# A linear-attention and gated-MLP kernel: the spatial products of the last batch as seven half-block products in place of eight

## The chip, the core and the metric

The kernel runs on one core of one Trainium2 chip. The metric is device time in microseconds: 328.46 (median of three runs, 327.94 to 328.81). One execution was also taken with the hardware profiler; it took 327.86 us.

## The reference

Four batches of 1088 tokens go through linear attention with four heads and then through a gated MLP in which the tokens are mixed. The MLP's input is the attention's output `x` of one batch, 1088 tokens x 128 channels:

```python
h = gelu(x @ w_in)                      # 1088 x 1024
u, v = h[..., :512], h[..., 512:]
v_n = (v - mean(v)) / sqrt(var(v) + 1e-6) * g_ln
v_s = einsum('ts,bsd->btd', w_sg, v_n) + b_sg[None, :, None]    # the spatial product
out = x + (u * v_s) @ w_out
```

The spatial product takes the weights `w_sg` (1088 x 1088), the same for all batches, times the normalized half `v_n` (1088 x 512). It is most of the arithmetic.

## The kernel before

All matrix products of the MLP are made from two-word numbers: each factor is held as a high word (a cast to `fp32r`) and a low word (what the cast left), and a product is three TensorE matmuls, high x high, high x low and low x high. In the names `w_h`, `w_l` are the words of the transposed spatial weights, `vh`, `vl` those of the normalized values.

**Tiles.** The 1088 input tokens are nine tiles `t` of 128 (the last is half full and is used as one matmul per word of the values). The 1088 output tokens are three chunks `ci` of 362, 362 and 364 columns (`CH`, line 23). The 512 gate features are four blocks `db` of 128. One spatial product of a block and a chunk, `pz_db_ci`, gathers in one PSUM bank over the nine tiles: 8 x 3 + 2 = 26 matmuls (`zs`, line 854). Batch 3 has 12 of them. Then follow, for each block and chunk, `gt` = z * g_ln + bias (`scale`, line 873, VectorE, one operand in PSUM), the product with `u` (`gate`, 882, VectorE), its two words `gh` (`g_h`, 886, ScalarE) and `gl` (`g_l`, 891, VectorE) and three matmuls into `po` (`out`, 904). `pu` (line 859) is the product for `u`, `pv` (717 to 744) that for the values; `vn` are the values, `v3` (line 815) normalizes a tile on ScalarE, `split_h` and `split_l` (823, 829) make the two words of a block, the first on ScalarE and the second on VectorE.

**Attention of batch b+1** runs beside the MLP of batch b. The names that matter here: `pk`, `pkv` and `pnd` are its matmuls; `kv_h`, `kv_l` the words of the key-value sums (lines 437, 439, VectorE), which `pnd` needs as weights; `e_0a`, `e_0b` and so on hold the query features, whose words are `qph` (ScalarE, line 509) and `qpl` (line 514). `qpl` is GpSimd's only regular work: six subtractions of two SBUF tiles for each of the batches 1 to 3.

**What sets the order.** The program is a list of about 1700 steps made by the functions at the end of the file. `WHEN` (line 36) holds one number for each step, and the steps are written into the program in the order of these numbers (`Steps.run`, line 137). Each engine then works through its own instructions in this order; semaphores between engines are set by the tiles that the steps write and read. Nothing is reordered at run time: an instruction that waits holds back all that stand behind it on its engine.

Of the kernel before, what the change touches and what calls it, by code (L numbers as in the profile page):

```python
# [120 lines left out]
]  # L121


def f32(ap):
# [4 lines left out]


# [993 lines left out]
```

## Time and profile before

| | |
|---|---|
| median of three runs | 328.46 us |
| profiled execution | 327.86 us |
| span of that execution, first to last instruction | 325.8 us |
| TensorE matmuls busy | 318.4 us, 98% of the span |
| VectorE, ScalarE, GpSimd busy | 251.6, 158.8, 22.8 us |
| granted TensorE clock | 1.0 of full speed throughout |

The last batch's spatial products start at 259 us of the span; the MLP of batch 2 and the attention of batch 3 run before and beside them. A busy PE means that matmuls are in its pipe: consecutive ones overlap, so the step from one start to the next is the better measure of what one costs.

### The profile page before, as it was taken

Reading aid. Unit: us, or ns where it says so; the run is one execution under the profiler, and the core shown is the slowest. Engines: PE = TensorE matmul, PEld = TensorE weight load, DVE = VectorE, ACT = ScalarE, POOL = GpSimd, SP = SyncE. Lnnn points to the kernel's source line nnn. Section 1 sums busy time; section 2 is a strip of 40 time slices with the busy share of each in tenths; the row PEclk is TensorE's granted clock in tenths of the full one; section 3 lists DMA queues with packets and bytes.
Section 4 is the critical chain, followed back from the end, with each engine's and each line's share of the span. In section 5 each row is a group of like instructions: output and inputs, shape, how many; then the busy total and the mean of one; then the engine's idle time right before and its main releaser. Section 6 shows DMA issues by size and latency. Waiting matters only on the chain.

```text
span 325.8 us, 5961 instructions
## 1 busy us (share of the span) xinstructions
PE 318.4 (98%) x2282; PEld 304.7 (93%) x2282; DVE 251.6 (77%) x614; ACT 158.8 (49%) x347; POOL 22.8 (7%) x35
## 2 busy tenths in 40 slices
PE   7999999999999999999999999999999999999995
PEld 5777999899999999999999999999999999999993
DVE  5899999999998967597988967768998874443243
ACT  4579714646549734354629815244634954131210
POOL 0300000022200000202200000112200000000000
PEclk9999999999999999999999999999999999999999
DMA  7999934774000115832000012551000000000002
GB/s 218 370 423 348 404 137 131 175 180 118 2 0 0 48 49 138 194 96 57 2 0 24 2 68 47 109 94 45 2 1 2 24 35 11 0 2 0 0 2 68
DMA packets 14091, 29.55 MB, mean 91 GB/s; under 512 B 1744, under 2 KB 10224, under 8 KB 13680
## 3 DMA queue, kind: packets, MB, share of 16 engines
q1 hardware_dynamic: 13344, 23.87, 25.1%
q0 software_dynamic: 720, 5.31, 4.3%
q8 instruction: 18, 0.29, 0.4%
q14 instruction: 9, 0.07, 0.1%
...
## 4 chain that ended last, share of the span: by engine, by line
PE 82%; DVE 11%; ACT 3%; DMA 2%; issue 1%; SPq 1%; ACTq 0%; DVEq 0%
PE pz L840 38%; PE pz L849 17%; PE pu L864 3%; DVE w_l L708 2%; PE po L913 2%; PE pu L866 2%; PE po L911 2%; PE pu L865 2%; PE po L910 2%; PE pkv L420 2%; PE pv L736 2%; PE pv L735 2%; PE pv L744 2%; DMA vn<-in_q 2%; PE pk L388 1%
## 5 line engine op out<-in xcount | busy, mean ns | idle before, releaser
L840 PE MATMUL pz<-w_h,vl 128*128 128x362 f32 (+1 forms) x432 | 140.1, 325 | 0.4 <-DVE vl L832 0.4
L840 PE MATMUL pz<-w_h,vh 128*128 128x362 f32 (+1 forms) x432 | 140.1, 325 | 0.0
L849 PE MATMUL pz<-w_l,vh 128*128 128x362 f32 (+1 forms) x384 | 118.0, 324 | 0.0
L840 PEld LDWEIGHTS pz<-w_h,vl 128*128 128x128 f32 x432 | 81.1, 188 | 1.4 <-DVE vl L832 0.9
L840 PEld LDWEIGHTS pz<-w_h,vh 128*128 128x128 f32 x432 | 81.1, 188 | 1.0 <-ACT u L871 0.3
L849 PEld LDWEIGHTS pz<-w_l,vh 128*128 128x128 f32 x384 | 71.1, 188 | 0.1
L877 DVE SCALAR_TENSOR_TENSOR gt<-pz,vi,b_bc 128x362 f32<-128x362 f32 (+3 forms) x49 | 28.5, 584 | 38.6 <-PE pz L840 38.3
L889 ACT CAST gh<-gt 128x362 fp32r<-128x362 f32 (+1 forms) x47 | 23.0, 493 | 53.6 <-DVE gt L884 49.8
L871 ACT ACTIVATE u<-pu 128x362 f32<-128x362 f32 (+1 forms) x48 | 22.7, 472 | 24.6 <-PE pu L866 16.2
L892 DVE TENSOR_TENSOR gl<-gt,gh 128x362 fp32r<-128x362 f32 (+1 forms) x47 | 26.4, 563 | 9.8 <-ACT gh L889 9.7
L827 ACT CAST vh<-vn 128x128 fp32r<-128x128 f32 (+1 forms) x72 | 25.8, 403 | 13.8 <-PE pz L840 13.4
L832 DVE TENSOR_TENSOR vl<-vn,vh 128x128 fp32r<-128x128 f32 (+1 forms) x72 | 28.5, 419 | 2.0 <-ACT vh L827 1.8
L817 ACT ACTIVATE vn<-vn,nm,rs 128x512 f32<-128x512 f32 x36 | 28.2, 811 | 2.6 <-DVE nm L811 2.5
L884 DVE TENSOR_TENSOR gt<-gt,u 128x362 f32<-128x362 f32 (+3 forms) x49 | 25.9, 528 | 0.9
L749 ACT ACTIVATE vn<-pv 128x512 f32<-128x512 f32 x36 | 21.0, 597 | 8.6 <-PE pv L744 7.7
L765 DVE BATCH_NORM_STATS2 st<-vn 128x6 f32<-128x512 f32 x33 | 22.5, 683 | 2.9 <-ACT vn L749 2.4
L535 DVE RECIPROCAL den<-den 128x362 f32<-128x362 f32 (+1 forms) x9 | 21.8, 2417 | 2.9 <-ACT den L530 2.9
L514 POOL TENSOR_TENSOR qpl<-e_0a,qph 128x362 fp32r<-128x362 f32 x6 | 6.5, 1103 | 145.2 <-ACT qph L509 145.2
L864 PE MATMUL pu<-x_h,win_h 128*128 128x362 f32 (+1 forms) x48 | 16.2, 338 | 0.0
L866 PE MATMUL pu<-x_l,win_h 128*128 128x362 f32 (+1 forms) x48 | 15.7, 327 | 0.0
L865 PE MATMUL pu<-x_h,win_l 128*128 128x362 f32 (+1 forms) x48 | 15.6, 326 | 0.0
L913 PE MATMUL po<-gl,wout_h 128*128 128x362 f32 (+1 forms) x47 | 15.5, 329 | 0.0
...
## 6 DMA issues: line engine op xcount, KB each, us to landing
...
```

The costliest lines, as they stand in the source:

```text
L765: V.bn_stats(st, self.vn[:, t])
L817: A.activation(self.vn[:, t], self.vn[:, t], AF.Identity, bias=self.nm[:, t : t + 1], scale=self.rs[:, t : t + 1])
L827: A.copy(self.parts[db][0][:, ts], self.vn[:, ts, P * db : P * db + P])
L832: V.tensor_sub(vl[:, ts], self.vn[:, ts, P * db : P * db + P], f32(vh[:, ts]))
L840: mm(self.z[db, ci], lhsT=self.parts[db][i][:, t], rhs=T["w_h"][:, t, AT[ci] : AT[ci] + cw], start=(t == 0 and i == 0), stop=(t == NT - 1 ...
L849: mm(self.z[db, ci], lhsT=self.parts[db][0][:, t], rhs=T["w_l", t][:, AT[ci] : AT[ci] + CH[ci][1]], start=False, stop=False,)
L864: mm(pu, lhsT=T["win_h"][:, ws], rhs=xh[:, cs], start=True, stop=False)
L871: A.activation(self.u[db, ci], self.pu.pop((db, ci)), AF.Gelu_apprx_tanh)
L877: V.scalar_tensor_tensor(self.gt[db, ci][:, s], self.z[db, ci][:, s], T["g_col"][:, db : db + 1], T["b_bc"][:, c0 : c0 + cw][:, s], op0=AL ...
L884: V.tensor_mul(gt, gt, self.u[db, ci][:, s])
L889: A.copy(self.g[db, ci][0], self.gt[db, ci])
L892: V.tensor_sub(self.g[db, ci][1], self.gt.pop((db, ci)), f32(self.g[db, ci][0]))
```

## The change

Batch 3 gets a class of its own, `Fast`, in place of `Gate`. For its blocks 0 and 2, and again for 1 and 3 (`PAIRS`), the tiles 0 to 3 and 4 to 7 and the chunks 0 and 1 make a product of two 2 x 2 matrices of half blocks (four tiles, one block, 362 columns: 12 matmuls each). Before, this took eight half-block products; now it is seven, of sums of half blocks, in Winograd's form of Strassen's method. The parts are:

- Sums of the weights (`Sums`): four for each of four tile pairs, `t1` to `t4`. The pieces of the weights are loaded anew from HBM by twelve DMAs on SyncE's queue (`ldT`), GpSimd makes the sums (`sum`, 16 instructions `T`), ScalarE their high words (`high`, 16) and GpSimd their low words (`rest`, 16). `t1` is stored over chunk 1 of tiles 0 to 3 in `w_h` and `w_l`; the others use tiles of the attention that are free by then.
- Sums of the values: `s1` to `s4` for each pair, on VectorE and in place in `vn` (`sums`, 8 instructions), and their words.
- The words of the values are made by half blocks (`word_h`, `word_l`) and for tile 8 alone (`edge`).
- The products `x`, `v`, `w`, `u` gather in one bank each. VectorE takes a bank out between (`take`: bank * g_ln + what was gathered before, which lies in SBUF), ten times for a pair, where `scale` stood four times.
- Chunk 2 (`third`) and tile 8 (`rest` of `Fast`) are as before in number.
- The order is new from the 1137th step on, in the middle of batch 2's MLP: the numbers in `WHEN` from the 1109th on are others; here one line of them.

```diff
+PAIRS = ((0, 2), (1, 3))
...
-    1116, 1119, 1121, 1125, 1128, 1192, 1051, 1088, 1118, 1122, 1124, 1127, 1129, 1132, 1133, 1135, 1136, 1138,
+    1116, 1119, 1121, 1125, 1128, 1273, 1051, 1088, 1118, 1122, 1124, 1127, 1129, 1132, 1133, 1135, 1153, 1159,
...
+    class Fast(Gate):
...
+        def word_h(self, j, n, t0, k):
+            A.copy(self.block(j, n)[:, 0, t0 : t0 + k], self.source(j, n)[:, t0 : t0 + k])
+
+        def word_l(self, j, n, t0, k):
+            w = self.block(j, n)
+            V.tensor_sub(w[:, 1, t0 : t0 + k], self.source(j, n)[:, t0 : t0 + k], f32(w[:, 0, t0 : t0 + k]))
+
...
+        def sums(self, j, n):
+            d1, d2 = PAIRS[j]
+            a11, a12, a21, a22 = (self.half(d, k) for d in (d1, d2) for k in range(2))
+            o, x, y, op = {
+                "s1": (a22, a21, a22, ALU.add), "s3": (a21, a11, a21, ALU.subtract),
+                "s2": (a22, a22, a11, ALU.subtract), "s4": (a12, a12, a22, ALU.subtract),
+            }[n]
+            V.tensor_tensor(o, x, y, op=op)
+
...
+        def product(self, j, o, left, right, t, first):
+            p = self.open((j, o))[:, : CH[0][1]]
+            w = self.words[j, left]
+            h, l = self.right(right, t)
+            mm(p, lhsT=w[:, 0, t], rhs=h, start=first, stop=False, **GO)
+            mm(p, lhsT=w[:, 0, t], rhs=l, start=False, stop=False, **GO)
+            mm(p, lhsT=w[:, 1, t], rhs=h, start=False, stop=t == 3, **GO)
+
+        def rest(self, j, o, db, ci):
+            p = self.open((j, o))[:, : CH[0][1]]
+            for i in range(2):
+                mm(
+                    p, lhsT=self.words[db][:, i], rhs=T["w_h"][:, NT - 1, AT[ci] : AT[ci] + CH[ci][1]],
+                    start=False, stop=i == 1, **GO,
+                )
+
+        def take(self, j, o, db, ci, first, final):
+            c0, cw = CH[ci]
+            z, add = self.open((j, o))[:, :cw], T["b_bc"][:, c0 : c0 + cw]
+            if not first:
+                add = self.acc[db, ci]
+            if final:
+                to = self.gt[db, ci] = new([P, CW], "gt", f"gt{self.b}_{db}_{ci}")[:, :cw]
+            elif first:
+                i = db // 2 if ci else 2
+                to = self.acc[db, ci] = T["vx"].rearrange("p n c -> p (n c)")[:, WP * i : WP * i + cw]
+            else:
+                to = add
+            V.scalar_tensor_tensor(to, z, T["g_col"][:, db : db + 1], add, op0=ALU.mult, op1=ALU.add)
+
...
+    class Sums:
...
+        def load(self, t, u):
+            if u == 0:
+                self.raw[t] = new([P, 3 * WP], "kld", f"wr{t}")
+                load(self.raw[t][:, : 2 * WP], wd[:, t, : 2 * WP])
+            elif u == 1:
+                load(self.raw[t][:, 2 * WP :], wd[:, t + 4, WP : 2 * WP])
+            else:
+                self.raw[t, 3] = new([P, WP], "wa", f"wa{t}")
+                load(self.raw[t, 3], wd[:, t + 4, :WP])
+
...
+        def sum(self, n, t):
+            x, y, op = {
+                "t3": ("b22", "b12", ALU.subtract), "t1": ("b12", "b11", ALU.subtract),
+                "t2": ("t3", "b11", ALU.add), "t4": ("b21", "t2", ALU.subtract),
+            }[n]
+            G.tensor_tensor(self.of(n, t), self.of(x, t), self.of(y, t), op=op)
+
...
+        def high(self, n, t):
+            if n == "t1":
+                cs = slice(AT[1], AT[1] + CH[1][1])
+                T[n, t] = T["w_h"][:, t, cs], T["w_l", t][:, cs]
+            else:
+                T[n, t] = [w[:, : CH[0][1]] for w in self.place(n, t)]
+            A.copy(T[n, t][0], self.of(n, t))
+
+        def rest(self, n, t):
+            h, l = T[n, t]
+            G.tensor_sub(l, self.of(n, t), f32(h))
...
     def gated(g, db, ci):
         if (db, ci) == g.final:
             return last(g, db, ci)
-        at(("gt", g.b, db, ci), lambda: g.scale(db, ci))
+        if not (isinstance(g, Fast) and ci < 2):
+            at(("gt", g.b, db, ci), lambda: g.scale(db, ci))
         at(("gm", g.b, db, ci), lambda: g.gate(db, ci))
         at(("gh", g.b, db, ci), lambda: g.g_h(db, ci))
         at(("gl", g.b, db, ci), lambda: g.g_l(db, ci))
...
+    def fast(g):
+        w = Sums()
+        for t in range(4):
+            for u in range(3):
+                at(("ldT", t, u), lambda t=t, u=u: w.load(t, u))
+            for n in ("t3", "t1", "t2", "t4"):
+                at(("T", n, t), lambda n=n, t=t: w.sum(n, t))
+            for n in ("t3", "t2", "t4"):
+                at(("Th", n, t), lambda n=n, t=t: w.high(n, t))
+                at(("Tl", n, t), lambda n=n, t=t: w.rest(n, t))
+        for t in range(4):
+            at(("Th", "t1", t), lambda t=t: w.high("t1", t))
+            at(("Tl", "t1", t), lambda t=t: w.rest("t1", t))
+        def pair(j, d1, d2):
+
+            def words(n, step):
+                for t in range(0, 4, step):
+                    at(("vh", g.b, j, n, t), lambda t=t: g.word_h(j, n, t, step))
+                    at(("vl", g.b, j, n, t), lambda t=t: g.word_l(j, n, t, step))
+
+            def products(o, left, right, first):
+                for t in range(4):
+                    at(("p", g.b, j, o, left, t), lambda t=t: g.product(j, o, left, right, t, first and t == 0))
+
+            def taken(o, db, ci, first=False, final=False):
+                if final:
+                    at(("gt", g.b, db, ci), lambda: g.take(j, o, db, ci, first, True))
+                    gated(g, db, ci)
+                else:
+                    at(("tk", g.b, j, o, db, ci), lambda: g.take(j, o, db, ci, first, False))
+
+            def rest(o, db, ci):
+                at(("p8", g.b, j, o, db, ci), lambda: g.rest(j, o, db, ci))
+
+            def third(db):
+                unit(g, db, 2)
+                for t in range(NT):
+                    at(("z", g.b, db, 2, t), lambda t=t: g.third(db, t))
+                gated(g, db, 2)
+
+            a11, a12, a21, a22 = ((d, k) for d in (d1, d2) for k in range(2))
+            for n in (a11, a12):
+                words(n, 4 if j else 1)
+            at(("vh", g.b, j, 8, d1), lambda: g.edge_h(d1))
+            at(("vl", g.b, j, 8, d1), lambda: g.edge_l(d1))
+            third(d1)
+            products("x", a11, (0, 0), True)
+            for n in (a21, a22):
+                words(n, 4)
+            at(("vh", g.b, j, 8, d2), lambda: g.edge_h(d2))
+            at(("vl", g.b, j, 8, d2), lambda: g.edge_l(d2))
+            for db, ci in ((d1, 1), (d2, 0), (d2, 1)):
+                taken("x", db, ci, first=True)
+            products("x", a12, (1, 0), False)
+            rest("x", d1, 0)
+            unit(g, d1, 0)
+            taken("x", d1, 0, first=True, final=True)
+            if not j:
+                third(d2)
+            products("v", a22, "t4", True)
+            rest("v", d2, 0)
+            taken("v", d2, 0)
+            at(("s", g.b, j, "s1"), lambda: g.sums(j, "s1"))
+            words("s1", 4)
+            for n in ("s3", "s2", "s4"):
+                at(("s", g.b, j, n), lambda n=n: g.sums(j, n))
+            words("s4", 4)
+            products("w", "s1", "t1", True)
+            taken("w", d2, 1)
+            products("w", "s4", (1, 1), False)
+            rest("w", d1, 1)
+            taken("w", d1, 1)
+            words("s2", 4)
+            products("u", "s2", "t2", True)
+            unit(g, d1, 1)
+            taken("u", d1, 1, final=True)
+            words("s3", 4)
+            products("u", "s3", "t3", False)
+            unit(g, d2, 0)
+            taken("u", d2, 0, final=True)
+            rest("u", d2, 1)
+            unit(g, d2, 1)
+            taken("u", d2, 1, final=True)
+            if j:
+                third(d2)
+
+        for j, (d1, d2) in enumerate(PAIRS):
+            pair(j, d1, d2)
...
     for b in range(1, B):
         attend(b)
-        g = Gate(b)
+        g = (Fast if b == B - 1 else Gate)(b)
         normed(g, GROUPS[1])
         if b == B - 1:
             for i in range(4):
                 at(("prep", i), lambda i=i, g=g: g.prepare(i))
-        main(g, 0)
+        if b == B - 1:
+            fast(g)
+        else:
+            main(g, 0)
```

On TensorE this is a stretch of batch 3 before, with `pu` of block 0 and chunk 1, the end of batch 2's last product and the first triple of batch 3's first one:

```order
L864 MATMUL pu_0_1_3353<-x_h,win_h 128x362
L865 MATMUL pu_0_1_3353<-x_h,win_l 128x362
L866 MATMUL pu_0_1_3353<-x_l,win_h 128x362
L840 MATMUL pz_3_2_3290<-w_h,vh_3_2869 128x364
L840 MATMUL pz_3_2_3290<-w_h,vl_3_2870 128x364
L840 MATMUL pz_0_0_3364<-w_h,vh_0_3307 128x362
L840 MATMUL pz_0_0_3364<-w_h,vl_0_3308 128x362
L849 MATMUL pz_0_0_3364<-w_l_710,vh_0_3307 128x362
```

And this is what stands behind the same `pu` now (`wb` are words of half blocks of values, `wt1t4` the words of sum `t4` of tile pair 1):

```order
L872 MATMUL pu_0_1_3520<-x_h,win_h 128x362
L873 MATMUL pu_0_1_3520<-x_h,win_l 128x362
L874 MATMUL pu_0_1_3520<-x_l,win_h 128x362
L1010 MATMUL pz_(0, 'x')_3354<-w_h,wb_04_3344 128x362
L1011 MATMUL pz_(0, 'x')_3354<-w_l_737,wb_04_3344 128x362
L1012 MATMUL pz_(0, 'x')_3354<-w_h,wb_04_3344 128x362
L1010 MATMUL pz_(0, 'v')_3461<-wt1t4h,wb_06_3422 128x362
L1011 MATMUL pz_(0, 'v')_3461<-wt1t4l,wb_06_3422 128x362
L1012 MATMUL pz_(0, 'v')_3461<-wt1t4h,wb_06_3422 128x362
L1010 MATMUL pz_(0, 'w')_3509<-w_h,wb_0s_3487 128x362
L1011 MATMUL pz_(0, 'w')_3509<-w_l_668,wb_0s_3487 128x362
L1012 MATMUL pz_(0, 'w')_3509<-w_h,wb_0s_3487 128x362
```

A product is still three matmuls of 362 columns; the products of several banks now take turns, triple by triple.

GpSimd's list from the attention of batch 3 to the end, before (`MEMSET kv` clears the key-value sums):

```order
L429 MEMSET kv_2724 128x256
L514 TENSOR_TENSOR qpl_0_2793<-e_0a,qph_0_2792 128x362
L514 TENSOR_TENSOR qpl_1_2826<-e_0a,qph_1_2825 128x362
L514 TENSOR_TENSOR qpl_2_2916<-e_1a,qph_2_2915 128x362
L514 TENSOR_TENSOR qpl_3_2961<-e_1a,qph_3_2960 128x362
L514 TENSOR_TENSOR qpl_4_3006<-e_2a,qph_4_3005 128x364
L514 TENSOR_TENSOR qpl_5_3052<-e_2a,qph_5_3051 128x364
```

And the same place now (`wr`, `wa` and `vi` hold pieces and sums of the weights, line 1095 makes a sum and line 1120 a low word):

```order
L439 MEMSET kv_2697 128x256
L1095 TENSOR_TENSOR wr_2581<-wr_2581 128x362
L1095 TENSOR_TENSOR vi<-wr_2581 128x362
L524 TENSOR_TENSOR qpl_1_2772<-e_0a,qph_1_2771 128x362
L524 TENSOR_TENSOR qpl_0_2784<-e_0a,qph_0_2783 128x362
L1095 TENSOR_TENSOR wr_2581<-wr_2581 128x362
L1120 TENSOR_TENSOR wt0t3l_2769<-wr_2581,wt0t3h 128x362
L524 TENSOR_TENSOR qpl_3_2877<-e_1a,qph_3_2876 128x362
L1120 TENSOR_TENSOR wt0t2l_2883<-wr_2581,wt0t2h 128x362
L524 TENSOR_TENSOR qpl_2_2864<-e_1a,qph_2_2863 128x362
L1095 TENSOR_TENSOR wa_2874<-wa_2874,wr_2581 128x362
L1095 TENSOR_TENSOR wr_2965<-wr_2965 128x362
```

The 32 new subtractions and additions of two SBUF tiles stand between the six of the attention and behind them; the last of them is read a little past the middle of batch 3's products.

VectorE's list at the key-value words of batch 3, before:

```order
L437 CAST kv_h<-kv_2724 128x256
L476 TENSOR_TENSOR ab_1_2654<-pab_1_2603,ab_1_2654 64x362
L439 TENSOR_TENSOR kv_l<-kv_2724,kv_h 128x256
L832 TENSOR_TENSOR vl_2_2594<-vn_2030,vh_2_2593 128x384
L458 TENSOR_TENSOR qt_2l<-q_2_2307,qt_2h 128x364
```

And now, with the two feature products `e_1a`, `e_0a` and the gating of block 0's chunk 2 between the two words:

```order
L447 CAST kv_h<-kv_2697 128x256
L513 TENSOR_TENSOR e_1a<-e_1a,e_1b 128x362
L513 TENSOR_TENSOR e_0a<-e_0a,e_0b 128x362 x2
L885 SCALAR_TENSOR_TENSOR gt_0_2_2790<-pz_0_2_2678,vi,b_bc 128x364
L840 TENSOR_TENSOR vl_2_2781<-vn_2031,vh_2_2780 128x384
L892 TENSOR_TENSOR gt_0_2_2790<-gt_0_2_2790,u_0_2_2498 128x364
L885 SCALAR_TENSOR_TENSOR gt_1_2_2812<-pz_1_2_2609,vi,b_bc 128x364
L486 TENSOR_TENSOR ab_2_2761<-pab_2_2754,ab_2_2761 64x364
L449 TENSOR_TENSOR kv_l<-kv_2697,kv_h 128x256
```

`kv_l` moved behind seven other instructions, and on TensorE the first `pnd` that reads it stands 24 matmuls behind the last one of `pz_0_2`, whose bank the `gt_0_2` row takes.

## Rows read from the trace of the kernel before

**Rows 1.** The page: busy us of each engine, share of the span, instructions.
```profile
PE 318.4 (98%) x2282; PEld 304.7 (93%) x2282; DVE 251.6 (77%) x614; ACT 158.8 (49%) x347; POOL 22.8 (7%) x35
```

**Rows 2.** Stretches of 10 us: us, then busy time of PE, PEld, DVE, ACT, POOL.
```profile
205.00:215.00 10.00, 10.00 (x63) 10.00 (x63) 7.94 (x16) 2.81 (x6) 2.21 (x2) 1.00 0.66 115
215.00:225.00 10.00, 10.00 (x64) 10.00 (x63) 6.74 (x10) 5.10 (x11) 0.97 (x1) 1.00 0.25 77
225.00:235.00 10.00, 10.00 (x61) 9.74 (x60) 9.57 (x18) 5.35 (x12) 2.93 (x3) 1.00 0.01 2
235.00:245.00 10.00, 10.00 (x60) 9.60 (x59) 9.23 (x18) 4.62 (x10) 0.00 (x0) 1.00 0.00 1
245.00:255.00 10.00, 10.00 (x58) 9.47 (x57) 8.36 (x33) 5.23 (x10) 0.00 (x0) 1.00 0.01 2
255.00:265.00 10.00, 10.00 (x64) 10.00 (x63) 8.28 (x27) 9.28 (x23) 0.00 (x0) 1.00 0.10 37
265.00:275.00 10.00, 10.00 (x64) 10.00 (x63) 5.25 (x11) 3.42 (x8) 0.00 (x0) 1.00 0.06 20
```

**Rows 3.** Timeline of PE late in batch 3: start us, us, instruction.
```profile
309.80 0.32 PE L840 MATMUL pz<-w_h,vh 128*128 128x362 f32 x1
...
311.24 0.32 PE L840 MATMUL pz<-w_h,vl 128*128 128x362 f32 x1
```

**Rows 4.** Groups of VectorE by form, 200 to 326 us: busy us, mean ns | idle before.
```profile
L877 DVE SCALAR_TENSOR_TENSOR gt<-pz,vi,b_bc 128x362 f32<-128x362 f32 x14 | 8.3, 594 | 16.1 <-PE pz L840 16.0
L892 DVE TENSOR_TENSOR gl<-gt,gh 128x362 fp32r<-128x362 f32 x14 | 8.1, 581 | 5.4 <-ACT gh L889 5.4
L884 DVE TENSOR_TENSOR gt<-gt,u 128x362 f32<-128x362 f32 x14 | 7.5, 535 | 0.4
L832 DVE TENSOR_TENSOR vl<-vn,vh 128x384 fp32r<-128x384 f32 x13 | 6.6, 550 | 0.0
...
L439 DVE TENSOR_TENSOR kv_l<-kv,kv_h 128x256 fp32r<-128x256 f32 x1 | 0.4, 425 | 0.0
```

**Rows 5.** Timeline of all engines at the end, 317.5 to 326 us.
```profile
318.84 0.33 PE L840 MATMUL pz<-w_h,vl 128*128 128x364 f32 x1
...
319.20 0.72 DVE L877 SCALAR_TENSOR_TENSOR gt<-pz,vi,b_bc 128x184 f32<-128x184 f32 x2 [1.93 <-PE pz L840]
...
322.00 0.35 DVE L926 TENSOR_TENSOR o<-pl,o 128x184 f32<-128x184 f32 x1
```

**Rows 6.** Timeline of GpSimd, 157.2 to 159.2, 210 to 212, 212.6 to 214.5, 233 to 234 us.
```profile
157.71 1.01 POOL L514 TENSOR_TENSOR qpl<-e_2a,qph 128x364 fp32r<-128x364 f32 x1 [1.32 <-issue]
...
210.34 0.97 POOL L514 TENSOR_TENSOR qpl<-e_0a,qph 128x362 fp32r<-128x362 f32 x1 [51.37 <-ACT qph L509]
...
212.81 1.24 POOL L514 TENSOR_TENSOR qpl<-e_0a,qph 128x362 fp32r<-128x362 f32 x1 [1.50 <-ACT qph L509]
...
232.52 0.98 POOL L514 TENSOR_TENSOR qpl<-e_2a,qph 128x364 fp32r<-128x364 f32 x1 [2.79 <-ACT qph L509]
```

**Rows 7.** Timeline of VectorE, the same four stretches.
```profile
157.35 0.53 DVE L548 TENSOR_TENSOR x_l<-den,x_h 128x362 fp32r<-128x362 f32 x1
157.80 1.31 DVE L892 TENSOR_TENSOR gl<-gt,gh 128x362 fp32r<-128x362 f32 x1
...
210.63 1.07 DVE L892 TENSOR_TENSOR gl<-gt,gh 128x362 fp32r<-128x362 f32 x1 [0.39 <-ACT gh L889]
...
212.69 0.54 DVE L884 TENSOR_TENSOR gt<-gt,u 128x362 f32<-128x362 f32 x1
213.84 0.61 DVE L892 TENSOR_TENSOR gl<-gt,gh 128x362 fp32r<-128x362 f32 x1 [0.62 <-ACT gh L889]
...
232.80 0.60 DVE L877 SCALAR_TENSOR_TENSOR gt<-pz,vi,b_bc 128x362 f32<-128x362 f32 x1
233.31 0.59 DVE L892 TENSOR_TENSOR gl<-gt,gh 128x362 fp32r<-128x362 f32 x1
```

More of the change, by code (lines that the diff above doesn't have):

```diff
@@ L31 @@
 SUMS = (0,1,2)
+PAIRS = ((0, 2), (1, 3))
+GO = dict(skip_group_check=True)
 WARM = 14
@@ L256, in load_k0 @@
         if part == 0:
+            const("pad_k", [P, 40])
             T["k0"] = new([P, SP], "kld", "k0")
@@ L280, in w_f @@
     def w_f(t):
+        if "pad_w" not in T:
+            const("pad_w", [P, 40])
         if ("w_f", t) not in T:
@@ L291, in gate_wh @@
     def gate_wh():
-        G.tensor_copy(new([P, 40], "wait", "wait", I32)[:, :1], T["vi"].bitcast(I32)[:, :1])
+        G.tensor_copy(new([P, 64], "wait", "wait", I32)[:, :1], T["vi"].bitcast(I32)[:, :1])
     def gate_wf():
@@ L447, in load_q @@
             c0, cw = CH[ci]
-            self.q[ci] = q = new([P, CW], "q", f"q{self.b}_{ci}")
+            self.q[ci] = q = new([P, WP], "q", f"q{self.b}_{ci}")
             load(q[:, :cw], qd[self.b, :, c0 : c0 + cw])
@@ L895, in prepare @@
             if i == 0:
-                self.wf = new([P, C], "kld", "wout_f")
+                self.wf = new([P, C], "kp", "wout_f")
                 V.tensor_add(self.wf, f32(T["wout_h"][:, NB - 1]), f32(T["wout_l"][:, NB - 1]))
@@ L934, in store, with __init__, half, block @@
             load(outd[self.b, :, c0 : c0 + cw][:, s], self.o[ci][:, s])
+    class Fast(Gate):
+        SLOT = dict(s1="vh", s2="vh", s3="vl", s4="vl")
+        def __init__(self, b):
+            super().__init__(b)
+            self.words, self.acc, self.bank, self.n = {}, {}, {}, {}
+        def half(self, db, k):
+            return self.vn[:, 4 * k : 4 * k + 4, P * db : P * db + P]
+        def block(self, j, n):
+            if (j, n) not in self.words:
+                tag = self.SLOT[n] if n in self.SLOT else "vl" if n[1] else "vh"
+                self.words[j, n] = new([P, 2, NT // 2, P], tag, f"wb{self.b}_{j}{n if n in self.SLOT else n[0] + 4 * n[1]}", F32R)
+            return self.words[j, n]
+        def edge(self, db):
+            if db not in self.words:
+                self.words[db] = new([P, 2, P], "kb", f"we{self.b}_{db}", F32R)
+            return self.words[db]
+        def source(self, j, n):
+            d1, d2 = PAIRS[j]
+            return self.half(*{"s1": (d2, 1), "s2": (d2, 1), "s3": (d2, 0), "s4": (d1, 1)}.get(n, n))
+        def word_h(self, j, n, t0, k):
[3 more added lines that the diff above has]
+            V.tensor_sub(w[:, 1, t0 : t0 + k], self.source(j, n)[:, t0 : t0 + k], f32(w[:, 0, t0 : t0 + k]))
+        def edge_h(self, db):
+            A.copy(self.edge(db)[:, 0], self.vn[:, NT - 1, P * db : P * db + P])
+        def edge_l(self, db):
+            w = self.edge(db)
+            V.tensor_sub(w[:, 1], self.vn[:, NT - 1, P * db : P * db + P], f32(w[:, 0]))
+        def sums(self, j, n):
+            d1, d2 = PAIRS[j]
+            a11, a12, a21, a22 = (self.half(d, k) for d in (d1, d2) for k in range(2))
[4 more added lines that the diff above has]
+            V.tensor_tensor(o, x, y, op=op)
+        def right(self, n, t):
+            if n[0] == "t":
+                return T[n, t]
+            k, ci = n
+            cs = slice(AT[ci], AT[ci] + CH[ci][1])
+            return T["w_h"][:, 4 * k + t, cs], T["w_l", 4 * k + t][:, cs]
+        def open(self, o):
+            if o not in self.bank:
+                self.bank[o] = bank(f"pz{self.b}_{o}")
+            return self.bank[o]
+        def product(self, j, o, left, right, t, first):
[25 more added lines that the diff above has]
+            V.scalar_tensor_tensor(to, z, T["g_col"][:, db : db + 1], add, op0=ALU.mult, op1=ALU.add)
+        def third(self, db, t):
+            j, m = db % 2, db // 2
+            ci = len(CH) - 1
+            cs = slice(AT[ci], AT[ci] + CH[ci][1])
+            if t == 0:
+                self.z[db, ci] = bank(f"pz{self.b}_{db}_{ci}")[:, : CH[ci][1]]
+            if t == NT - 1:
+                for i in range(2):
+                    mm(self.z[db, ci], lhsT=self.words[db][:, i], rhs=T["w_h"][:, t, cs], start=False, stop=i == 1)
+                return
+            w = self.words[j, (db, t // 4)]
+            for q, (i, r) in enumerate(((0, T["w_h"][:, t]), (0, T["w_l", t]), (1, T["w_h"][:, t]))):
+                mm(self.z[db, ci], lhsT=w[:, i, t % 4], rhs=r[:, cs], start=(t == 0 and q == 0), stop=False)
+        def out(self, db, ci):
+            cw = CH[ci][1]
+            k = self.n[ci, "o"] = self.n.get((ci, "o"), 0) + 1
+            if k == 1:
+                self.po[ci] = bank(f"po{self.b}_{ci}")[:, :cw]
+            o = self.po[ci]
+            gh, gl = self.g.pop((db, ci))
+            mm(o, lhsT=T["wout_h"][:, db], rhs=gh, start=(k == 1), stop=False)
+            mm(o, lhsT=T["wout_l"][:, db], rhs=gh, start=False, stop=False)
+            mm(o, lhsT=T["wout_h"][:, db], rhs=gl, start=False, stop=k == NB - (ci == len(CH) - 1))
@@ new lines, in tile_kernel, with __init__, of, place @@
+    class Sums:
+        HOME = (("s", "s", "q"), ("e", "e", "ab"), ("e", "e", "r"), ("x", "x", "x"))
+        def __init__(self):
+            self.raw, self.space = {}, {}
+        def load(self, t, u):
[7 more added lines that the diff above has]
+                load(self.raw[t, 3], wd[:, t + 4, :WP])
+        def of(self, n, t):
+            if n == "t1" and t < 3:
+                w = T["vx"].rearrange("p n c -> p (n c)")[:, WP * t : WP * t + WP]
+            elif n in ("b21", "t4"):
+                w = self.raw[t, 3]
+            else:
+                i = {"b11": 0, "t2": 0, "b12": 1, "t1": 1, "b22": 2, "t3": 2}[n]
+                w = self.raw[t][:, WP * i : WP * i + WP]
+            return w[:, : CH[0][1]]
+        def sum(self, n, t):
[4 more added lines that the diff above has]
+            G.tensor_tensor(self.of(n, t), self.of(x, t), self.of(y, t), op=op)
+        def place(self, n, t):
+            i = int(n[1]) - 2
+            tag = self.HOME[t][i]
+            if tag == "e":
+                w = new([P, 2 * WP], "e", f"wt{t}{n}", F32R)
+                return w[:, :WP], w[:, WP:]
+            if tag == "x":
+                for k in range(2):
+                    if ("x", k) not in self.space:
+                        self.space["x", k] = new([P, 3 * WP], "x", f"wt{t}{k}", F32R)
+                return [self.space["x", k][:, WP * i : WP * i + WP] for k in range(2)]
+            return [new([P, WP], tag, f"wt{t}{n}{k}", F32R) for k in "hl"]
+        def high(self, n, t):
[8 more added lines that the diff above has]
+            G.tensor_sub(l, self.of(n, t), f32(h))
@@ L980, in normed @@
                 at(("v3", g.b, t), lambda t=t: g.v3(t))
+                if isinstance(g, Fast):
+                    continue
                 at(("vh", g.b, 0, t), lambda t=t: g.split_h(0, t, 1))
@@ L1077, in tile_kernel @@
                 at(("prep", i), lambda i=i, g=g: g.prepare(i))
-        main(g, 0)
+        if b == B - 1:
+            fast(g)
+        else:
+            main(g, 0)
     steps.run(tc)
```

4 lines of the change are left out of this document (1 added, 3 removed), and 71 rows, old and new, of the table WHEN.

## The prediction

> **What bounds the kernel now.** I read the table of busy times first. TensorE's matmuls fill 98% of the span, VectorE 77%, ScalarE 49%, GpSimd 7% [rows 1]. A busy matmul engine could still wait, so I went to the stretches: from 205 to 275 us, where batch 2's MLP, batch 3's attention and then batch 3's MLP run, PE is busy for 10.00 of every 10 us [rows 2], and the table of waits has no wait of PE from 200 us to the end. So in this half of the kernel the time is the number of matmuls times the step between two of them. That step is in the timeline: nine steps from 309.80 to 311.24, 0.16 us each for 362 columns [rows 3]; the 0.32 us that a row gives as duration is twice that, since each runs under its neighbour. The other engines need only be in time. What has to be watched is whether they stay so: VectorE is idle for only 14.6 of the 70 us (70 less the seven busy times, 55.4) [rows 2].
>
> The run to which the sums are made took 327.86 us, a span of 325.8 and 2.1 around it. It lies 0.6 under the median of 328.46, so a result worked out from it is raised by 0.6 for the forecast.
>
> **What the change removes.** Two pairs, each with one half-block product fewer: 2 x 4 tiles x 3 = 24 matmuls of 362 columns. Tile 8 and chunk 2 keep their matmuls. 24 x 0.16 = 3.8 us off the path, since PE has nothing else to wait for there. This much is sure if PE still never waits.
>
> **What it adds off the path.** ScalarE gets 24 casts. Those of 362 or 512 columns are on an engine that is half idle over the seven stretches (35.8 of 70 us busy) though full in one, 9.28 of 10 us at 255 [rows 2]; cost 0, and up to 0.5 where words are late there. Twelve DMAs, 3.1 MB in all, stand on SyncE's queue, where DMA is idle from 225 to 255 us [rows 2]; each sum is read long after its load in the order, cost 0. Each product bank of kind `x` must be emptied by three `take` before TensorE writes on. For the first pair 53 other matmuls, 8.5 us, stand between in the order; three rows like `gt` from a bank take 3 x 0.59 [rows 4], so hidden. At the end the last product is followed by twelve matmuls in place of nine, but the tail goes through VectorE: from the last product's start at 318.84 to the last addition at 322.00 are 3.2 us [rows 5]. The u-product now stands in it, so the gate could come later; bounds -0.2 and +0.5, taken as 0, since matmuls run on beside it as now.
>
> VectorE gets 28 instructions of some 0.5 to 0.6 us [rows 4]: eight sums, twelve more bank reads, and low words cut differently. About half stand before GpSimd's last new result is needed: 7 us, so of its 14.6 us of idle time about 7.6 remain in that stretch.
>
> **The cost that decides: GpSimd against VectorE.** GpSimd had six subtractions in this stretch and now has 38 operations of two SBUF tiles; at 0.97 us [rows 6] they fill 37 us, half of the some 70. What happens when the two engines meet is in the trace. A `gl` that starts at 157.80, while GpSimd works from 157.71 to 158.72, takes 1.31 us in place of 0.53. Another at 210.63, against GpSimd 210.34 to 211.31, takes 1.07 [rows 6, 7]. In both the end is 0.39 after GpSimd's end. The one at 233.31 also ends 0.4 after GpSimd's end (233.50), and so does that at 213.84. The other way round, GpSimd's row at 212.81 takes 1.24, ending 0.83 after the VectorE row that began before it. But `gt<-pz` at 232.80, which reads one tile of SBUF and one of PSUM, is 0.60 beside GpSimd, its usual time [rows 4, 7]. So VectorE's operations of two SBUF tiles and GpSimd's exclude each other.
>
> The Trainium skill has this rule (SBUF — State Buffer, section "Who interferes with whom"): a VectorE instruction with two SBUF inputs and a GpSimd instruction that reads SBUF share one read interface, and the later of the two is fully blocked until the first has ended. By that rule, and the trace agrees with its 1.31 against 0.53 us, no collision is partly paid; a sum that took GpSimd's work as free because the engine was idle at 7% would give 324.6 us here.
>
> The price of one collision: alone the VectorE row ends 0.53 after its start; in a collision it ends 0.39 after GpSimd's end. If it starts at any point of the 0.97 us, the loss is on average 0.97/2 + 0.39 - 0.53 = 0.35 us, at most 0.83. In the new order I count 69 such VectorE rows in the stretch (from the `e_1a` row to the last words of `s3` of the first pair). 69 x 0.5 x 0.35 = 12 us; before, the same stretch lost 0.54 + 0.07 + 0.05 = 0.7 (the three rows at 210, 214 and 233 us). So VectorE gets 11.4 us more of waiting.
>
> How much of that does PE see? At least what VectorE's idle time can't hold: 11.4 - 7.6 = 3.8. A place worked out for the rest: `kv_l`. From the last matmul of `pz_0_2` to the first `pnd` that needs `kv_l` there are 24 others, 24 x 0.16 = 3.8 us. VectorE's `gt_0_2` starts 0.36 after that matmul's start (318.84 to 319.20 in [rows 5]), and six rows have to go through: 0.51 + 0.47 + 0.45 + 0.51 + 0.45 + 0.43 = 2.8 (the durations of [rows 4], less the 0.08 by which the next row starts early, as at 157.35 and 157.80 in [rows 7]; `ab` as the gate). Spare: 0.7. Three of them, `vl`, the gate and `kv_l`, read two SBUF tiles, while GpSimd has four operations one behind the other, 3.9 us. So each meets one: 0 to 0.83, say 0.5; 1.5 of delay, 0.8 of PE wait. Thus somewhat over half gets through, 0.55 x 11.4 = 6.3. Between 3.8 and 6.3 I take 4.5, nearer to the first, because the kernel's other hand-overs are mostly behind the end of a product, with idle time before them (16.0 us of it before `gt`, [rows 4]). For the range I keep 0 (all of it falls into idle time, 14.6 in all) and 8.5 (three quarters get through).
>
> **Sum.** 327.86 - 3.8 + 4.5 = 328.5; for the median 329.1, forecast 329.0 us. The gain of the matmuls is eaten by a wait that didn't exist.
>
> **Rivals.**
>
> 1. *The delays are hidden.* VectorE's collisions fall where it would have waited for PE anyway, and PE's waits stay under 2.9 us. For: 16.0 us of VectorE's idle time stand before `gt` alone [rows 4], and the whole `gl` group lost little, 581 against 535 ns [rows 4]. Against: collisions were rare, since GpSimd had 6 operations in 120 us. It would give 328.46 - 3.8 = 324.6, or up to 327.4 with what remains.
>
> 2. *Slower: the low words come just in time.* The same exclusion, but at TensorE's weights: each product triple's third matmul reads a low word that VectorE makes by an operation of two SBUF tiles, and `s1` to `s4` are made by such ones too. If the new order hands most of them over with less than 0.35 us to spare, three quarters of the waits come through: 8.5, and 328.46 - 3.8 + 8.5 = 333.2. It turns to slower from 4.8 us of PE waits on. For it: in 225 to 245 VectorE had only 1.2 us idle [rows 2], so there nothing absorbs a delay, and what is late once stays late. Against: after GpSimd's last result (past the middle of batch 3's products) nothing collides and no more is lost.
>
> 3. *The change doesn't save 24 matmuls.* The trace would show that in the count; the order has 24 fewer, so I give it nothing.
>
> **How the numbers follow.** The forecast, PE waits of 3 to 6 us: 0.45, with a range of its own from 327.6 to 330.6. Rival 1: 0.27. Rival 2: 0.28. A measurement of this kernel tells 0.3%, 1.0 us, from no change. The forecast's case lies mostly within that (0.35 of 0.45), and 0.10 of it above. So faster 0.27, same 0.35, slower 0.38. The range reaches into both rivals, from 325.2 (rival 1 with 0.6 us of waits) to 332.2 (rival 2 with 7.5 us), and leaves out 0.1 on either side.
>
> **What would show it.** Right: 24 matmuls fewer; idle time of PE between 205 and 285 us of 3 to 6 us in all, before `pnd` with `kv_l` and before triples with `wb`, released by VectorE; rows of `vl`, `gl`, gate and `wb` of 0.9 to 1.3 us beside GpSimd rows, and rows from PSUM unchanged; GpSimd rows of up to 1.3. Wrong: those long rows, but PE's waits under 3 us (rival 1), or VectorE rows of 0.53 throughout (the exclusion doesn't hold here). If PE waits for GpSimd or a DMA itself, or in the second half of batch 3, I have overlooked something else.

## The result, and the profile after

| | us | ratio to the kernel before (95%) |
|---|---|---|
| before, in the same runs | 327.91 | |
| changed kernel | 331.63 | 1.011 (1.0085 to 1.0136) |

The change makes the kernel 1.1% slower, 3.7 us; the forecast was 329.0 (range 325.2 to 332.2), with 0.38 on slower. The profiled execution took 332.57 us, with a span of 330.8.

TensorE did what the sum took off: 2258 matmul rows in place of 2282, 24 fewer. But it is no longer always busy. These are stretches of the changed kernel, with the columns of [rows 2] (us, then busy time of PE, PEld, DVE, ACT, POOL, the granted clock, the share of DMA and its GB/s):

```profile
205.00:215.00 10.00, 8.87 (x55) 8.57 (x53) 5.16 (x8) 3.94 (x9) 3.85 (x4) 1.00 0.27 68
215.00:225.00 10.00, 9.19 (x47) 9.19 (x48) 8.26 (x13) 4.00 (x9) 4.21 (x5) 0.83 0.57 129
...
255.00:265.00 10.00, 8.08 (x46) 7.09 (x45) 9.68 (x29) 7.68 (x17) 2.83 (x3) 1.00 0.19 61
265.00:275.00 10.00, 9.33 (x53) 8.10 (x52) 9.98 (x17) 6.23 (x15) 5.98 (x5) 1.00 0.07 20
```

PE lacks 1.1, 0.8, 1.9 and 0.7 us in these, and VectorE is full from 255 to 275 (9.68 and 9.98 of 10). The table of waits of PE from 190 us on names who was waited for (total us, times, longest):

```profile
PE pnd L532 <- DVE kv_l L449: 1.9, 1, 1.9
PE pz_(0, 'x')_3354 L1012 <- DVE wb L976: 1.7, 1, 1.7
PE po L921 <- DVE gl L900: 0.5, 2, 0.3
PE pz_(0, 'v')_3461 L1012 <- DVE wb L976: 0.4, 1, 0.4
PE pl L925 <- DVE gt L892: 0.2, 1, 0.2
```

All are waits for VectorE, 4.7 us; in the kernel before the table has none from 200 us on. Here is how the largest but one arises. VectorE's timeline (start us, us), then GpSimd's beside it:

```profile
258.11 0.59 DVE L885 SCALAR_TENSOR_TENSOR gt<-pz,vi,b_bc 128x362 f32<-128x362 f32 x1
258.62 0.61 DVE L812 TENSOR_TENSOR nh<-nh,nv 128x4 f32<-128x4 f32 x1
259.26 0.90 DVE L813 TENSOR_SCALAR np<-nh 128x4 f32<-128x4 f32 x1
260.08 1.38 DVE L900 TENSOR_TENSOR gl<-gt,gh 128x362 fp32r<-128x362 f32 x1
261.38 0.15 DVE L814 TENSOR_TENSOR np<-np,nh 128x4 f32<-128x4 f32 x1
...
262.08 0.28 DVE L976 TENSOR_TENSOR wb<-vn,wb 128x128 fp32r<-128x128 f32 x1
```

```profile
258.23 1.90 POOL L1120 TENSOR_TENSOR wt2t<-wr,wt2t 128x362 fp32r<-128x362 f32 x2 [4.35 <-ACT wt2t L1116]
260.09 0.97 POOL L1095 TENSOR_TENSOR wa<-wa,wr 128x362 f32<-128x362 f32 x1
```

`gl` ends at 261.46, 0.40 after GpSimd's end at 261.06, as in [rows 6, 7]; `gt`, with an operand in PSUM, keeps its 0.59. New to me are the rows of four elements: alone they take 0.15 to 0.17, here 0.61 and 0.90, ending 0.02 and 0.03 after GpSimd's two low words (at 259.21 and 260.13; the row shows both as one). `wb` stands behind them all, and TensorE waited for it from 260.6 on. The other large wait, `kv_l`, VectorE and then GpSimd:

```profile
207.38 0.54 DVE L513 TENSOR_TENSOR e_0a<-e_0a,e_0b 128x362 f32<-128x362 f32 x1 [4.18 <-DMA e_0a<-ab]
209.94 0.54 DVE L513 TENSOR_TENSOR e_0a<-e_0a,e_0b 128x362 f32<-128x362 f32 x1 [2.02 <-DMA e_0b<-e_0d]
...
211.45 1.08 DVE L840 TENSOR_TENSOR vl<-vn,vh 128x384 fp32r<-128x384 f32 x1 [0.34 <-ACT vh L835]
212.46 1.30 DVE L892 TENSOR_TENSOR gt<-gt,u 128x364 f32<-128x364 f32 x1
...
214.85 0.90 DVE L449 TENSOR_TENSOR kv_l<-kv,kv_h 128x256 fp32r<-128x256 f32 x1
```

```profile
211.15 2.21 POOL L524 TENSOR_TENSOR qpl<-e_0a,qph 128x362 fp32r<-128x362 f32 x2 [10.08 <-ACT qph L519]
213.32 1.25 POOL L1095 TENSOR_TENSOR wr<-wr 128x362 f32<-128x362 f32 x1
214.53 0.95 POOL L1120 TENSOR_TENSOR wt0t3l<-wr,wt0t3h 128x362 fp32r<-128x362 f32 x1
```

Two things come together: the row in front waits until 209.94 for a DMA, and then three rows of some 0.5 us are blocked, by 0.53, 0.77 and 0.48. The first two stand beside `qpl`, which the kernel before has too; only the third stands beside a new operation. On TensorE that reads:

```profile
213.54 0.32 PE L531 MATMUL pnd<-qph,kv_h 128*128 128x362 f32 x1
215.81 0.44 PE L532 MATMUL pnd<-qph,kv_l 128*128 128x362 f32 x1 [1.94 <-DVE kv_l L449]
216.08 0.33 PE L533 MATMUL pnd<-qpl,kv_h 128*128 128x362 f32 x1
...
216.98 0.51 PE L848 MATMUL pz<-w_h,vl 128*128 128x362 f32 x1
217.28 0.50 PE L857 MATMUL pz<-w_l,vh 128*128 128x362 f32 x1
```

The row behind the wait is followed after 0.27 in place of 0.16, and from 216.98 ten steps are 0.30 and the next is 0.27: half clock (1.2 GHz), in the stretch whose granted clock is 0.83. That is 10 x 0.14 + 0.11 = 1.5 us in this execution. The other five had a mean clock of 1.0 (this one 0.993) and took 330.53 to 331.89.

The account of the profiled execution: -3.8 for the matmuls; 4.7 of waits; 1.5 of half clock; the rest, some 2.3 to the 4.7 us by which it is longer, lies around the stops (a stop costs 0.16 more than its idle time, and the next step is 0.11 longer than usual) and in steps too short for the table (the first matmuls of `pv` and `po`, 0.1 to 0.2 more each).

### The profile page after: what moved, and what is told of

The parts are those of the page before. It is cut to its first block, busy times and chain, and to the rows that moved or that the text cites. A ratio compares the mean times of both kernels' runs of the same rounds, so it can differ in the third digit from the quotient of the medians.

```text
span 330.8 us, 6058 instructions
## 1 busy us (share of the span) xinstructions
PE 319.2 (96%) x2258; PEld 302.1 (91%) x2258; DVE 277.7 (84%) x642; ACT 168.5 (51%) x371; POOL 55.5 (17%) x67
## 4 chain that ended last, share of the span: by engine, by line
PE 61%; DVE 19%; issue 7%; DMA 5%; ACT 3%; SPq 2%; POOL 1%; ACTq 0%; DVEq 0%; POOLq 0%
PE pz L848 20%; PE pz L857 9%; PE pz L1048 4%; DVE w_l L716 2%; DVE gt L892 2%; DMA w_f<-in_w 2%; DVE st L773 2%; DMA vi<-in_v 2%; PE pu L872 2%; PE pu L874 2%; PE pu L873 2%; DMA e_0b<-e_0d 2%; PE po L921 2%; DVE vl L840 1%; PE po L918 1%
## 5 line engine op out<-in xcount | busy, mean ns | idle before, releaser
L848 PE MATMUL pz<-w_h,vh 128*128 128x362 f32 (+1 forms) x324 | 106.2, 328 | 0.2 <-ACT u L879 0.2
L848 PE MATMUL pz<-w_h,vl 128*128 128x362 f32 (+1 forms) x324 | 105.9, 327 | 0.4 <-DVE vl L840 0.4
L857 PE MATMUL pz<-w_l,vh 128*128 128x362 f32 (+1 forms) x288 | 87.5, 326 | 0.0
L848 PEld LDWEIGHTS pz<-w_h,vl 128*128 128x128 f32 x324 | 61.4, 190 | 1.6 <-DVE vl L840 0.9
L848 PEld LDWEIGHTS pz<-w_h,vh 128*128 128x128 f32 x324 | 61.4, 189 | 1.4 <-ACT u L879 0.5
L857 PEld LDWEIGHTS pz<-w_l,vh 128*128 128x128 f32 x288 | 53.5, 189 | 0.1
L835 ACT CAST vh<-vn 128x128 fp32r<-128x128 f32 (+1 forms) x54 | 19.6, 403 | 9.2 <-PE pz L848 8.8
L840 DVE TENSOR_TENSOR vl<-vn,vh 128x128 fp32r<-128x128 f32 (+1 forms) x54 | 23.0, 443 | 1.5 <-ACT vh L835 1.3
L1048 PE MATMUL pz<-w_h,wb 128*128 128x364 f32 x64 | 19.5, 327 | 0.0
L1095 POOL TENSOR_TENSOR wr<-wr 128x362 f32<-128x362 f32 x9 | 9.9, 1104 | 42.9 <-DMA e_1d<-ab 39.0
```

What stands on the lines that cost most here:

```text
L840: V.tensor_sub(vl[:, ts], self.vn[:, ts, P * db : P * db + P], f32(vh[:, ts]))
L848: mm(self.z[db, ci], lhsT=self.parts[db][i][:, t], rhs=T["w_h"][:, t, AT[ci] : AT[ci] + cw], start=(t == 0 and i == 0), stop=(t == NT - 1 ...
L857: mm(self.z[db, ci], lhsT=self.parts[db][0][:, t], rhs=T["w_l", t][:, AT[ci] : AT[ci] + CH[ci][1]], start=False, stop=False,)
L1048: mm(self.z[db, ci], lhsT=w[:, i, t % 4], rhs=r[:, cs], start=(t == 0 and q == 0), stop=False)
```

## The experiments

Theory 1: GpSimd's 32 new operations block VectorE, which then hands words to TensorE late (1a: only blocked rows that TensorE reads next cost; 1b: a fixed share of what is lost comes through). Theory 2: DMAs of the weights make VectorE's list late. Theory 3: VectorE simply has more to do. Ratios are to the kernel before, run beside each; it took 327.5 to 328.7 there, so the ratios compare two runs better than their times do.

| run | us | ratio (95%) |
|---|---|---|
| e1 sums and low words as memsets | 324.87 | 0.992 (0.989 to 0.994) |
| e2 as copies | 325.62 | 0.994 (0.992 to 0.996) |
| e3 `kv_l` early | 330.22 | 1.009 (1.005 to 1.012) |
| e4 before, 24 matmuls fewer | 324.74 | 0.991 (0.988 to 0.993) |
| e5 other order | 330.47 | 1.008 (1.005 to 1.011) |
| e6 memsets, loads late | 329.70 | 1.006 (1.003 to 1.008) |
| e7 low words as memsets | 327.57 | 1.000 (0.998 to 1.002) |
| e8 third order | 326.36 | 0.995 (0.993 to 0.997) |
| e9 memsets, `kv_l` early | 324.47 | 0.989 (0.986 to 0.992) |

**e1, memsets.** GpSimd writes the same places and reads nothing; the sums and their low words are left out.

```diff
-            G.tensor_tensor(self.of(n, t), self.of(x, t), self.of(y, t), op=op)
+            G.memset(self.of(n, t), 0.01)
...
-            G.tensor_sub(l, self.of(n, t), f32(h))
+            G.memset(f32(l), 0.001)
```

> The changed kernel, but GpSimd's 16 sums and 16 low words of the weights are memsets of the same 128x362 places: GpSimd writes them and reads nothing. VectorE's, ScalarE's, SyncE's and TensorE's lists stay as they are; only the values of T are not the sums. Theory 1 (GpSimd and VectorE exclude each other): VectorE's rows go back to 0.53 us, PE's waits of 4.7 us between 205 and 285 us shrink to under 1, and the time is 327.9 - 3.8 + 0.5 to 1.5 = 324.6 to 325.6 us. Theory 2 (VectorE's list is late because its e_0a products wait for DMAs that stand behind 576 KB of weights): the wait of pnd for kv_l stays over 1.5 us, 326 to 328.5. Theory 3 (VectorE simply has more to do, 28 instructions): no change, 330.5 to 332.

Measured 324.87, 6.8 us under the changed kernel (6.3 by the ratios). VectorE, ScalarE and SyncE have all their new work, so theory 3 falls, and with it any price of the casts, takes and DMAs that stands out of the noise. VectorE's rows of two SBUF tiles run beside a memset at their usual time; this is GpSimd, then VectorE, at one place:

```profile
258.92 0.41 POOL L1120 MEMSET w_l<- 128x362 f32 x1
```

```profile
258.81 0.53 DVE L900 TENSOR_TENSOR gl<-gt,gh 128x362 fp32r<-128x362 f32 x1
259.26 0.53 DVE L892 TENSOR_TENSOR gt<-gt,u 128x362 f32<-128x362 f32 x1
```

One wait stays beside the 0.2 at the end, `pnd` for `kv_l`, 1.3 us where under 1 was expected: beside `vl` and the gate two `qpl`, which the kernel had before, still block these rows (1.08 and 1.30 us). (A memset is also shorter, 0.40 us.)

**e2, copies.**

```diff
+            G.tensor_copy(self.of(n, t), self.of(x, t))
...
+            G.tensor_copy(l, self.of(n, t))
```

> The changed kernel, but GpSimd's 32 operations are copies: each reads one SBUF tile in place of two and writes the same place (so T is not the sums). Theory 1 in the form of the Trainium skill (SBUF - State Buffer, Who interferes with whom: a VectorE operation with two SBUF inputs against a GpSimd instruction that reads SBUF): the long VectorE rows stay, each ending 0.4 us after the copy, and the time lies between that of the memsets and 331.6 by the length of a copy. If only two operations of two inputs exclude each other: as the memsets, 324.6 to 325.6. Theory 3: 330.5 to 332.

Neither side had it whole. The time, 325.62, is that of the second; by the length of a copy, half a subtraction, it would have been some 328. The rows are those of the first: a copy reads one tile and blocks all the same. GpSimd (the first of its three copies ends at 259.86, the second at 260.59), then VectorE:

```profile
259.17 2.32 POOL L1095 COPY wr<-wr 128x362 f32<-128x362 f32 x3 [12.33 <-DMA wr<-in_w]
```

```profile
259.42 0.82 DVE L892 TENSOR_TENSOR gt<-gt,u 128x362 f32<-128x362 f32 x1
260.16 0.97 DVE L976 TENSOR_TENSOR wb<-vn,wb 128x512 fp32r<-128x512 f32 x1
```

So the rule of the Trainium skill (SBUF — State Buffer, section "Who interferes with whom"), that what counts is whether GpSimd's instruction reads SBUF, agrees with the trace, for a copy and for a memset. But a copy that meets nothing takes 0.49 us, half a subtraction, and the cost here was 325.62 - 324.87 = 0.8, a ninth of 6.8: the loss is far from proportional to GpSimd's time. The prediction's price of a collision gives the reason: with 0.49 in place of 0.97 it is 0.49/2 + 0.39 - 0.53 = 0.1 us in place of 0.35. In the traces from 200 us on, VectorE's rows beside GpSimd lose 3.1 us in all here, 1.6 with the memsets and 12.9 in the changed kernel (each against the shortest row of its operation and shape, where it is over 0.1 us longer; rows that read a bank left out).

**e3, `kv_l` early.** One number of `WHEN`: the step stands behind `kv_h` again.

```diff
+WHEN = list(WHEN)
+for i, w in ((1324, 1185.5),):
+    WHEN[i] = w
```

> The changed kernel with one step moved: kv_l directly behind kv_h on VectorE, in front of the products e_1a and e_0a that wait for DMAs and of gt_0_2, vl and the gate. Theory 1 and 2 alike: PE's wait of 1.9 us before pnd is gone, and with it the 2.1 us step and the eleven matmuls at 0.30 us (half clock) behind it where they showed; the waits at 258 to 275 us stay. 331.6 - 2.1 = 329.5, range 328.8 to 330.2. Theory 3: what is late once is late elsewhere, 331 to 332.

330.22, a gain of 1.4 where 2.1 were expected; by the ratios it is 0.8, and their intervals overlap, so the trace has to decide. The wait for `kv_l` is gone, but 0.8 of it came back at the next word of the same product; PE's waits:

```profile
PE pz_(0, 'x')_3354 L1016 <- DVE wb L980: 1.5, 1, 1.5
PE pnd L537 <- POOL qpl L528: 0.8, 1, 0.8
PE pv L747 <- DVE den L553: 0.6, 1, 0.6
```

**e4, the value of the matmuls.** An edit to the kernel before, which leaves out the third matmul of 24 triples.

```diff
+            if self.b == B - 1 and db < 3 and ci == 0 and t < NT - 1:
+                return
             self.z_lo(db, ci, t)
```

> The kernel before with 24 matmuls of 362 columns left out in batch 3 (the third of each triple, blocks 0 to 2, chunk 0, tiles 0 to 7), nothing else: the value of the matmuls alone. If each is worth its step: 327.9 - 24 x 0.16 = 324.1 us, 323.8 to 324.5. If other engines set the end: over 326.

By the ratio 3.1 us (2.2 to 3.9), its span is 322.0 against 325.8: the 3.8 stand at the edge of the interval. The median of 324.74 lies 0.2 above what was expected, and PE has a new wait of 0.4 us, for a `gl`.

**e5, another order** (new numbers in `WHEN` alone).

> The changed kernel with all its work, the same instructions on the same engines, in another order of the steps from the 1130th on: 537 steps stand elsewhere, most by 1 to 20 places and none by over 41. Moved are mostly VectorE's and ScalarE's word steps and GpSimd's sums and low words, so that what TensorE needs next is not behind a blocked operation. Theory 1a (what counts is where a collision falls: only late rows that TensorE reads next cost time): PE's waits after 200 us fall from 4.7 to under 1.5 us and the time to 324.5 to 326.5 us, under the kernel before. Theory 1b (what counts is how much the two engines lose in all, since VectorE is nearly full: a fixed share comes through in any order): 329 to 331.6 us.

A miss: 330.47. PE waited 1.4 us for a `vl`, since VectorE stood 5.0 us in front of it for the DMA of `e_0b` and the cast `kv_h` behind that was blocked (1.12 us in place of 0.29), and 1.2 and 1.0 for `wb`, once behind blocked rows of four elements and once because `wb` itself was blocked (1.44 us in place of 0.69). By this run alone 1b would stand.

**e6, loads late.** The memsets of e1, and `ldT` 0,0 and 0,1 behind the loads of `e_0a` and `e_0b`.

> The kernel with the 32 memsets, and the first two loads of weights (576 KB, in front of e_1d on SyncE's queue) moved behind the loads of e_0a and e_0b; values of T not the sums. Theory 2 (these loads make e_0a late, and kv_l with it): VectorE's wait of 4.2 us before the first e_0a row falls by 2 to 3.5, and the pnd wait of 1.3 us goes: 324.9 - 1.4 = 323.5. Against it (the qpl collisions beside vl and the gate, 0.55 + 0.77 us, make that wait, wherever they stand): e_0a earlier, but no more than 0.3 us gained, 324.6 to 325.2.

Worse than both sides expected, 329.70, and yet it answers the question: VectorE's wait before the first `e_0a` row is 3.7 us, not 4.2. The weights' loads don't make `e_0a` late. SyncE takes some 0.6 us for most of these issues (the two of `e_0a` 1.22), and the last `e_0b` is issued at 206.3, in the changed kernel at 206.6. The new waits came from ScalarE, where the cast of `t3` now held up what stands behind it:

```profile
211.72 0.49 ACT L1120 CAST wt0t3h<-wr 128x362 fp32r<-128x362 f32 x1 [2.18 <-POOL wr L1099]
212.12 0.49 ACT L523 CAST qph<-e_0a 128x362 fp32r<-128x362 f32 x1
212.52 0.51 ACT L839 CAST vh<-vn 128x384 fp32r<-128x384 f32 x1
```

TensorE waited for that `vh`, then for its `vl`, then for `kv_l`: 0.5, 0.7 and 1.5 us within 5 us. That is only some 1.4 us more than in e1, of 4.8; the clock cost more. Behind the waits eighteen steps of TensorE are 0.30, 18 x 0.14 = 2.5 us, in this stretch (columns as above):

```profile
215.00:225.00 10.00, 8.51 (x36) 8.22 (x34) 8.24 (x14) 3.02 (x7) 3.19 (x6) 0.66 0.56 126
```

All five executions of e6 have a mean clock under 1 (0.989 to 0.995). The edit changed more than it meant to.

**e7, half.** The 16 low words as memsets, the sums real.

> The changed kernel with the 16 low words of the weights as memsets and the 16 sums as they are (T's low words are not the real ones). Loss in proportion to GpSimd's operations that read SBUF: half of 331.6 - 324.9 = 6.7, so 328.2 us. If the loss starts only when the idle time of VectorE is used up (a threshold): 325.0 to 326.5. If the sums alone do it, since the kv_l and the first wb waits stand behind sums: 330 to 331.

327.57, between the proportion (328.2) and the threshold (325.0 to 326.5), so none of the three was met; 4.1 of the 6.8 us went with half of the operations. Counted as in e2, VectorE's rows lose 6.7 us here. In this one order the time above the memsets' thus goes with what these rows lose beyond the 1.6 there: 0.8 of 1.5 us with the copies, 2.7 of 5.1 here, 6.8 of 11.3 in the changed kernel, 0.5 to 0.6 of it each time.

**e8, a third order.** All work, `WHEN` alone.

> The changed kernel with all its work in a third order of the steps from the 1130th on (580 steps elsewhere, half of them by 5 places or less, none by over 69). It differs from the order of the run before last in what that one showed: VectorE's small operations (4 or 5 elements) are blocked by GpSimd as the large ones are, and the rows that need e_0b come some 3.3 us behind its issue; what TensorE reads next stands in front of both. Theory 1a (only the place of a collision counts): PE's waits after 200 us under 1.5 us, 324.5 to 326.5 us, faster than the kernel before. Theory 1b (a fixed share of what the two engines lose comes through in any order): 329 to 331.6 us.

326.36, faster than the kernel before by 0.5% (0.3 to 0.75) and, ratio by ratio, 1.6% or some 5 us faster than the changed one: 1b falls. PE's waits, 1.8 us where 1a expected under 1.5:

```profile
PE pnd L529 <- POOL qpl L520: 0.5, 1, 0.5
PE pz L1044 <- DVE wb L972: 0.3, 1, 0.3
PE pu L868 <- DVE gt L881: 0.3, 1, 0.3
PE pz L844 <- DVE den L545: 0.3, 1, 0.3
PE pz L844 <- DVE vl L836: 0.2, 1, 0.2
PE pl L921 <- DVE gt L888: 0.2, 1, 0.2
```

VectorE is blocked no less. Counted as in e2, the changed kernel loses 12.9 us in 21 rows, this one 13.2 in 23, the one with memsets 1.6 in 4. What differs is who is hit. VectorE at `kv_l`, and at the first `wb`:

```profile
212.57 0.41 DVE L445 TENSOR_TENSOR kv_l<-kv,kv_h 128x256 fp32r<-128x256 f32 x1
212.90 1.29 DVE L509 TENSOR_TENSOR e_1a<-e_1a,e_1b 128x362 f32<-128x362 f32 x1
214.12 1.30 DVE L896 TENSOR_TENSOR gl<-gt,gh 128x362 fp32r<-128x362 f32 x1
215.34 1.32 DVE L836 TENSOR_TENSOR vl<-vn,vh 128x384 fp32r<-128x384 f32 x1
...
254.14 0.89 DVE L790 TENSOR_SCALAR ny<-nv 128x4 int32<-128x4 int32 x1
254.95 0.28 DVE L972 TENSOR_TENSOR wb<-vn,wb 128x128 fp32r<-128x128 f32 x1
```

Three blocked rows of 1.3 us stand directly behind `kv_l`, and the word is in time; the first `wb` is made at 254.95 in place of 262.08.

**e9, both.** The memsets of e1 with the order of e3.

> The kernel with the 32 memsets and kv_l directly behind kv_h (values of T not the sums): both edits together. If the wait of pnd that was left with the memsets (1.3 us) is kv_l's place alone, it goes: 324.9 - 1.4 = 323.5 us, 323.0 to 324.0, the full 24 x 0.16 = 3.8 under the kernel before and a little more. If something else holds pnd then (qpl from GpSimd, as with kv_l early alone, 0.8 us): 324.3 to 324.9.

By ratio 1.1% under the kernel before, 3.5 of 3.8 us (the kernel before took 328.73 beside it, so the ratio counts). Apart from the 0.2 at the end PE waits once, 0.4 for `qpl`, as the second reading had it.

## Why the prediction was right, and where not

The forecast was 329.0, and 331.63 came: inside the range, but above the 327.6 to 330.6 of the forecast's own case, in the part that the range took from rival 2. The mechanism was right, the size of one term too small.

- **The matmuls, -3.8:** right. e4 has 3.1 (2.2 to 3.9), and e9, with every other part of the change but GpSimd's reads and with `kv_l` early, 3.5 (2.5 to 4.6).
- **Casts, takes, sums of values and DMAs at nothing:** right within the noise; e1 keeps them. The tail grew by 0.2: from the last product's start (324.19) to the last addition (327.58) 3.4 us, in place of 3.2 in [rows 5]; bounds were -0.2 and 0.5.
- **The exclusion and its price:** right. Blocked rows end 0.39 after GpSimd, rows from PSUM keep their time, and without the reads the time falls by 6.8. I counted 69 rows, half of them hit, 0.35 each: 12 us, 11.4 more than before. The trace has 12.9. That the two are so near is luck: only 21 rows are hit, at 0.61 each, and 3.6 us of it are in six rows of four or five elements, some with one SBUF input, so that the rule "two SBUF tiles" was too narrow.
- **How much comes through: the step that failed.** I took 4.5 between 3.8 and 6.3, "nearer to the first", because most hand-overs have idle time before them. It was 6.8 (331.63 - 324.87; 6.3 by the ratios). The 6.3 would have given 331.0. The idle time was not where the blocked rows are: of 10 us each VectorE has 4.8 idle from 205 to 215, but 0.3 in all from 255 to 275, where `wb` is late. My worked-out place pointed the same way and I had it too small: `kv_l` cost 1.9 us of wait, not 0.8, since I let its chain start with `gt_0_2`'s own product and overlooked that `gt_0_2` stands behind an `e_0a` row that waits for a DMA until 209.94. That row holds `gt_0_2` back by some 0.5, and `vl` by 0.3 more, since the words on ScalarE wait for it too; the three blocked rows lose 1.8 where I had 1.5. With the memsets 1.3 of the 1.9 stays, so most of this wait comes from the order and not from the new operations. The waits in the table, 4.7, are what I forecast; but a wait costs more than its row (some 0.3 around each, short gaps, in one execution the half clock), which my sum of waits left out. So the hit on the waits doesn't make the time right.
- **Rival 2** was nearer than the forecast in direction: slower, from low words that come just in time, `wb` among them. Its price, 8.5, was too high and its turning point, 4.8 us of waits in all, about where the table stands. Its place (words of the products) and mine (`kv_l`) cost about the same.
- **Rival 1** failed for this order but not in general: e8 hides nearly all of the same loss. So no share of a loss is a property of the work; "0.55 x 11.4" comes near the 6.8 in this order (0.5 to 0.6 in e2, e7 and the changed kernel) and far off in that of e8, with as much lost. The list of what stands between a blocked row and TensorE decides.

Not settled: why the clock fell to half behind the wait in one of six executions and not in the others, and why it fell in all five of e6. e8 lies 0.5% above e9, 1.8 us; its table of waits adds up to 1.8, that of e9 to 0.6.
